# Decode attention backward with one pass over K and V: the query gradient from M = sum of (V row)(p x K row)

## The chip, the cores and the metric

One core of one Trainium2 chip. The time is the device time of that core in microseconds; lower is better. Times of whole kernels are medians of several runs, and each experiment was timed beside runs of the kernel before on the same chip. Views of the profile and landings come from one profiled execution of each kernel. A landing is the moment when one of the 16 DMA engines has finished its share of a transfer; it is read from the semaphore events of the kept trace, which do not name the engine, so landings can only be put in order of time.

## The reference

A transformer layer with one new token per sequence: layer norm, attention over the last 4096 keys of a cache of 32768, output projection, layer norm, gated FFN, and the gradients of all inputs and weights.

```python
# B=2, D=512, Hq=32, Hkv=8, Sk=32768, Dh=128, F=1792; everything bf16
W = min(4096, max(256, Sk // 4)); rep = Hq // Hkv          # 4096 keys, 4 query heads per K/V head
q = (layernorm(x) @ wq).reshape(...)
k = repeat(k_cache[:, :, Sk - W:, :], rep);  v = repeat(v_cache[:, :, Sk - W:, :], rep)
p = softmax(einsum("bhqd,bhkd->bhqk", q, k) * Dh ** -0.5)
h = x + einsum("bhqk,bhkd->bhqd", p, v).reshape(...) @ wo
out = h + (gelu(layernorm(h) @ w_gate) * (layernorm(h) @ w_up)) @ w_down
# results: out, and the gradients of x, k_cache, v_cache, wq, wo, w_gate, w_up, w_down
```

The cache gradients have the cache's full size. Of each, 28672 of 32768 rows are zero, and they must be written: 32 regions of 7.34 MB, 235 MB of zeros.

## The kernel before

Zeros are written by GpSimd's queue from one small tile. Three regions are written by a second routine, which spares one DMA engine in each: 15 rows instead of 16. This is called a sparing below.

```python
SKIP_REGIONS = {6: (0, 1792), 14: (0, 1792), 22: (4, 1792)}     # region: (queue number, rows spared)
def zero_dma(i):                                                # plain: 128 partitions, 16 engines alike
    ...
    nc.gpsimd.dma_start(out=dst, in_=zt[:].unsqueeze(1).to_broadcast([P, nper, ZE]))
def zero_dma_skip(i, q, R=1792):
    ...                                                         # tiny writes that move the engines' order on
    nc.gpsimd.dma_start(out=flat[0:rem0].rearrange("(p k e) -> p k e", p=15, k=kd),
                        in_=zt[0:127:9, :].unsqueeze(1).to_broadcast([15, kd, ZE]))
    ...
```

K is read once for the scores and again for the query gradient:

```python
        def dq_for(bg):                                         # in the dV and dK stage
            Kb = kv_pool.tile([P, NJ, DH], BF16, tag="kv")
            ld_eng().dma_start(out=Kb[:], in_=Kv[:, bg, :, :])  # 1.05 MB, 16 times
            for j in range(NJ):
                c0 = (j // NJH) * NBH + bg * REP
                nc.tensor.matmul(out=dqT_ps[:, bg * REP:(bg + 1) * REP], lhsT=Kb[:, j, :],
                                 rhs=dsT2[:, j % NJH, c0:c0 + REP], start=(j == 0), stop=(j == NJ - 1))
```

V is read once for the output and 10 of its 16 tiles again for dP. All weights are loaded in long runs.

## Time and profile before

| | before |
|---|---|
| time, median (13 runs) | 864.78 us (864.47 to 865.36) |
| profiled span | 863.1 us |
| bytes moved / mean rate | 357.71 MB / 414 GB/s |
| last compute instruction ends / its last store lands | 682 us / 692 us |
| last zero write lands | 861.4 us |
| instructions | 8773 |

The span is a list of bytes at a nearly constant rate, with the compute beside it. The prediction below shows those lines. Two more lines of the page: the queues that fetch instructions (columns: packets, MB, share of 16 engines' time).

```profile
q8 instruction: 29, 0.48, 0.2%
q14 instruction: 12, 0.09, 0.0%
```

### The profile page before, as it was taken

What the parts mean: (1) busy time and instruction counts of PE and PEld (TensorE: products, weight loads), DVE (VectorE), ACT (ScalarE), POOL (GpSimd) and SP (SyncE); (2) the same over time, 40 slices, a digit from 0 to 9 for tenths busy, and PEclk for the clock granted to TensorE, in tenths of its full rate; (3) what the DMA queues carried; (4) which work ended last, traced back from release to release, by engine and by line L of the source; (5) the groups of instructions that cost most, each with busy time, mean ns of one, the idle gap of its engine ahead of it and who ended that gap; (6) DMA issues with size and microseconds to landing.
All of it is one profiled execution on the core that took longest, in us unless ns stands there. A gap on an engine that the chain in (4) does not pass through costs nothing.

```text
span 863.1 us, 8773 instructions
## 1 busy us (share of the span) xinstructions
PE 403.7 (47%) x3691; PEld 227.9 (26%) x3727; DVE 253.6 (29%) x402; ACT 216.3 (25%) x317; POOL 48.2 (6%) x67
## 2 busy tenths in 40 slices
PE   1527863244775949979744555567167200000000
PEld 1415543231543825544312222122032000000000
DVE  2202231000357456423423443567145200000000
ACT  0303441000225415534213333466123100000000
POOL 7000000000110000001010000000000010000000
PEclk9959995556677569976756776798677555555555
DMA  9999999999999999999999999999999999999995
GB/s 362 425 417 420 419 416 416 416 420 423 421 423 424 422 420 420 420 417 422 417 421 419 417 420 424 420 423 422 421 423 425 420 424 425 425 425 425 425 416 218
DMA packets 74809, 357.71 MB, mean 414 GB/s; under 512 B 3977, under 2 KB 3985, under 8 KB 61457
## 3 DMA queue, kind: packets, MB, share of 16 engines
q0 software_dynamic: 58480, 234.89, 72.9%
q1 hardware_dynamic: 13692, 103.38, 30.3%
q10 hardware_dynamic: 2596, 18.88, 5.2%
q8 instruction: 29, 0.48, 0.2%
q14 instruction: 12, 0.09, 0.0%
HBM read 74.72 MB, written 282.33 MB: 414 GB/s over the span
## 4 chain that ended last, share of the span: by engine, by line
another core or an unknown queue 76%; POOL 5%; issue 3%; POOLq 0%
POOL out_dram L107 3%; POOL out_dram L123 0%; POOL out_dram L121 0%; POOL zt L100 0%; POOL out_dram L136 0%; POOL out_dram L132 0%; POOL maskA L152 0%; POOLq L781 0%; POOL maskA L151 0%; POOL pair_f L159 0%; POOL out_dram L126 0%; POOL ident_bf L146 0%; POOL maskC L176 0%; POOL selB L180 0%
## 5 line engine op out<-in xcount | busy, mean ns | idle before, releaser
L70 DVE CAST st<-ps 128x512 bf16<-128x512 f32 (+1 forms) x136 | 92.6, 719 | 90.4 <-ACT st L72 58.5
L72 ACT CAST st<-ps 128x512 bf16<-128x512 f32 (+1 forms) x136 | 80.9, 612 | 105.1 <-PE ps L695 52.9
L301 PE MATMUL KT_ps<-ident_bf,Kb 128*128 128x128 bf16 x832 | 73.1, 234 | 43.8 <-DMA Kb<-in_A_k_cache_dram 42.6
L72 ACT COPY KT_sb<-KT_ps 128x1024 bf16<-128x1024 bf16 x64 | 64.8, 1012 | 104.6 <-PE KT_ps L301 104.6
L301 PEld LDWEIGHTS <-Kb 128*128 128x128 bf16 x832 | 58.4, 105 | 74.5 <-DMA Kb<-in_A_k_cache_dram 45.3
L70 DVE COPY KT_sb<-KT_ps 128x1024 bf16<-128x1024 bf16 x64 | 44.2, 691 | 106.6 <-PE KT_ps L301 89.8
L72 ACT COPY dst<-ps 128x512 bf16<-128x512 bf16 x53 | 31.0, 585 | 125.8 <-PE ps L244 49.7
L695 PE MATMUL ps<-dO_bd,p_bf 128*128 128x512 bf16 x119 | 43.4, 473 | 16.8 <-DVE st L70 15.8
L695 PE MATMUL ps<-Q_bd,ds_bf 128*128 128x512 bf16 x126 | 39.6, 410 | 23.2 <-DVE st L70 22.9
L107 POOL DMA_DIRECT2D out_dram<-zt x29 | 30.8, 1119 | 303.5 <-DMA out_dram<-zt 303.3
L311 PE MATMUL dP_ps<-KT_sb,dOpadX 128*128 128x512 bf16 x116 | 41.2, 430 | 3.8 <-DVE KT_sb L70 2.2
L70 DVE CAST g_st<-ps_gr 128x512 bf16<-128x512 f32 x39 | 26.9, 691 | 44.0 <-PE ps_gr L613 38.6
L311 PE MATMUL S_ps<-KT_sb,QpadX 128*128 128x512 bf16 x115 | 37.3, 397 | 5.0 <-ACT KT_sb L72 4.4
L72 ACT CAST g_st<-ps_gr 128x512 bf16<-128x512 f32 (+1 forms) x39 | 21.2, 544 | 57.4 <-PE ps_gr L613 57.2
L70 DVE COPY dst<-ps 128x512 bf16<-128x512 bf16 x53 | 22.7, 428 | 43.0 <-PE ps L244 31.3
L683 PE MATMUL dqT_ps<-dsT,Kb 128*128 128x4 bf16 x512 | 18.4, 167 | 34.7 <-DMA Kb<-in_A_k_cache_dram 33.7
L683 PEld LDWEIGHTS <-Kb 128*128 128x128 bf16 x512 | 17.4, 102 | 47.1 <-DMA Kb<-in_A_k_cache_dram 38.1
L428 PE MATMUL oT_ps<-pT,Vb 128*128 128x4 bf16 x416 | 13.1, 166 | 33.9 <-DMA Vb<-in_A_v_cache_dram 31.1
L695 PEld LDWEIGHTS <-ds_bf 128*128 128x128 bf16 x128 | 13.1, 102 | 49.7 <-issue 43.2
L244 PE MATMUL ps<-ident_bf,wq_full 128*128 128x128 bf16 x128 | 13.5, 234 | 24.3 <-ACT dst L72 19.8
L695 PEld LDWEIGHTS <-p_bf 128*128 128x128 bf16 x128 | 12.6, 111 | 36.0 <-issue 20.0
L428 PEld LDWEIGHTS <-Vb 128*128 128x128 bf16 x416 | 12.2, 104 | 35.1 <-DMA Vb<-in_A_v_cache_dram 32.1
(201 smaller groups left out, 421.5 us busy)
## 6 DMA issues: line engine op xcount, KB each, us to landing
out_dram<-zt POOLq DMA_DIRECT2D x29, 7168.0 KB, 124.9
Kb<-in_A_k_cache_dram SPq DMA_DIRECT2D x32, 1024.0 KB, 15.8
out_dram<-zt POOLq DMA_DIRECT2D x3, 6720.0 KB, 171.2
out_dram<-st SPq DMA_DIRECT2D x18, 1024.0 KB, 14.8
out_dram<-st ACTq DMA_DIRECT2D x18, 1024.0 KB, 18.1
Vb<-in_A_v_cache_dram SPq DMA_DIRECT2D x13, 1024.0 KB, 11.0
Kb<-in_A_v_cache_dram SPq DMA_DIRECT2D x10, 1024.0 KB, 10.3
out_dram<-g_st SPq DMA_DIRECT2D x5, 1792.0 KB, 15.2
```

The costliest lines, as they stand in the source:

```text
L70: nc.vector.tensor_copy(out=out, in_=in_)
L72: nc.scalar.copy(out=out, in_=in_)
L107: nc.gpsimd.dma_start(out=dst, in_=zt[:].unsqueeze(1).to_broadcast([P, nper, ZE]))
L244: nc.tensor.transpose(out=ps[:, a, :], in_=src_block(a), identity=ident_bf[:])
L301: nc.tensor.transpose(out=KT_ps[:, cc1, jj * P:(jj + 1) * P], in_=Kb[:, j, :], identity=ident_bf[:])
L311: nc.tensor.matmul(out=acc_ps[:, cc, :], lhsT=lhsT, rhs=KT_sb[:, cc1, :], start=(i < 2), stop=(i >= len(units) - 2))
L428: nc.tensor.matmul(out=oT_ps[:, bg * REP:(bg + 1) * REP], lhsT=Vb[:, j, :], rhs=pT2[:, j % NJH, c0:c0 + REP], start=(j == 0), stop=(j == N ...
L683: nc.tensor.matmul(out=dqT_ps[:, bg * REP:(bg + 1) * REP], lhsT=Kb[:, j, :], rhs=dsT2[:, j % NJH, c0:c0 + REP], start=(j == 0), stop=(j == ...
L695: nc.tensor.matmul(out=ps[:, half2, :], lhsT=lhs_bf[:, jp * P:(jp + 1) * P], rhs=rhs_bd[:, half2, bgq * 4:(bgq + 1) * 4, :].rearrange("q g ...
```

## The change

The intent: with delta known only after the output, ds = p(dP - delta), and dq = sum over keys of ds x K. Since dP = V dO, this is M dO - delta x pK, where M = sum over keys of (V row)(p x K row) and pK = sum of p x K. M and pK don't need dO, so they are summed in the same pass as the scores, and K need not come back. The core of the diff (cut; the whole replaces most tile pools by offsets into one tile):

```diff
+        def m_unit(bg, u, M_ps):                               # 4 of the 32 keys of each partition
+            ...
+            for jj in range(4):
+                for i in range(REP):
+                    if jj * REP + i in PK_ON_ACT:              # (2, 5, 8, 11, 14)
+                        nc.scalar.activation(out=pk[:, jj, i, :], in_=Kt[bg][:, j, :], func=ACT.Copy, scale=ef[:, j, i:i + 1])
+                    else:
+                        nc.vector.tensor_scalar(out=pk[:, jj, i, :], in0=Kt[bg][:, j, :], scalar1=ef[:, j, i:i + 1], ...)
+            ...
+                nc.tensor.matmul(out=M_ps[:], lhsT=Vt[bg][:, j, :], rhs=pk[:, jj, :, :]..., ...)
-            Kb = kv_pool.tile([P, NJ, DH], BF16, tag="kv")     # second read of K
-            ld_eng().dma_start(out=Kb[:], in_=Kv[:, bg, :, :])
-        if i in SKIP_REGIONS:
-            zero_dma_skip(i, *SKIP_REGIONS[i])
+        zero_cast(i)                                           # all 32 regions alike
+    wq2 = at(8 * V_SLOT, [P, NDR, HQ * DH], BF16, "wq2")       # wq read a second time
+    nc.sync.dma_start(out=wq2[:], in_=wq_v)
-        3: lambda: nc.sync.dma_start(out=wo_sb[:], in_=A_wo.rearrange("(p r) n -> p r n", r=NOR)),
+    wo_v = A_wo.rearrange("(h d) n -> d h n", h=HQ)            # 1 KB runs; FFN weights and gwd likewise
...
```

V now stays in 12 slots, so 4 tiles are read again in place of 10.

## The prediction

> **What bounds the kernel now.** I read the page first: the rows of slices for the DMA, then the queues and the bytes.
>
> ```profile
> PE   1527863244775949979744555567167200000000
> DVE  2202231000357456423423443567145200000000
> DMA  9999999999999999999999999999999999999995
> ...
> DMA packets 74809, 357.71 MB, mean 414 GB/s; under 512 B 3977, under 2 KB 3985, under 8 KB 61457
> ...
> q0 software_dynamic: 58480, 234.89, 72.9%
> q1 hardware_dynamic: 13692, 103.38, 30.3%
> q10 hardware_dynamic: 2596, 18.88, 5.2%
> ...
> HBM read 74.72 MB, written 282.33 MB: 414 GB/s over the span
> ```
>
> The DMA row is 9 in every slice but the last, while TensorE and VectorE have nothing after slice 33. So the kernel is a list of bytes to be moved: 235 MB of zeros for the untouched part of the two cache gradients (q0, issued by GpSimd) and 122 MB of everything else. The chain of waits says the same in its own way: three quarters of it is "another core or an unknown queue", that is, GpSimd waiting for its zero writes.
>
> Second, the table of stretches (columns: stretch, length, busy time of PE, PEld, DVE, ACT, POOL, granted clock, DMA share, GB/s). I set the borders where the stages change: K scores, V products, FFN, dP with the weight gradients, dV and dK, the last projection, zeros alone, the end.
>
> ```profile
> 0.00:136.00 136.00, 73.00 (x779) 51.32 (x793) 33.52 (x63) 38.73 (x45) 17.10 (x33) 0.87 1.05 410
> 136.00:187.00 51.00, 16.97 (x525) 15.66 (x523) 0.50 (x2) 1.09 (x2) 0.52 (x1) 0.50 1.07 416
> 187.00:300.00 113.00, 73.17 (x730) 50.91 (x731) 43.84 (x81) 33.24 (x45) 10.01 (x11) 0.67 1.15 423
> 300.00:414.00 114.00, 94.14 (x672) 50.52 (x682) 55.61 (x77) 46.00 (x60) 5.83 (x6) 0.82 1.12 421
> 414.00:608.00 194.00, 108.97 (x799) 45.06 (x809) 93.63 (x146) 79.74 (x143) 4.70 (x6) 0.74 1.07 420
> 608.00:690.00 82.00, 37.44 (x193) 14.44 (x192) 26.51 (x37) 17.46 (x24) 4.77 (x5) 0.64 1.11 423
> 690.00:836.00 146.00, 0.00 (x0) 0.00 (x0) 0.00 (x0) 0.00 (x0) 5.30 (x5) 0.50 1.14 425
> 836.00:863.00 27.00, 0.00 (x0) 0.00 (x0) 0.00 (x0) 0.00 (x0) 0.00 (x0) 0.50 0.68 255
> ```
>
> Two things to see. The compute chain ends at 690, so it has some 170 us of slack. And the last 27 us run at 255 instead of 425 GB/s: some DMA engines have finished and others have not, which costs 27 x (1 - 255/425) = 10.8 us.
>
> **What the Trainium skill says.** "DMA: Bandwidth & Descriptors", section "Issuing engines are not separate DMA queues": transfers issued by SP, ACT and GpSimd run on the same 16 engines and interleave. The trace agrees: 410 to 425 GB/s whatever the mix. So a byte not moved anywhere is worth time, as long as the zeros can fill the place. Same page, "Queues, rings and completion order": an engine takes its queues in turn. In the V stage the timeline has one 1 MB tile (1.049 MB) every 3.92 us, 267 of the 416 GB/s, so loads get about two thirds and the zeros still move:
>
> ```profile
> 153.40 1.01 PE L428 MATMUL oT_ps<-pT,Vb 128*128 128x4 bf16 x32 [2.91 <-DMA Vb<-in_A_v_cache_dram]
> 157.35 1.01 PE L428 MATMUL oT_ps<-pT,Vb 128*128 128x4 bf16 x32 [2.94 <-DMA Vb<-in_A_v_cache_dram]
> 161.26 0.93 PEld L428 LDWEIGHTS <-Vb 128*128 128x128 bf16 x32 [2.98 <-DMA Vb<-in_A_v_cache_dram]
> ```
>
> "VectorE: DVE Perf Modes", section "The perf-mode tier table": tensor_scalar on bf16 in SBUF runs at four elements a cycle. The four calls on 128x512 fit:
>
> ```profile
> 134.20 1.14 DVE L410 TENSOR_SCALAR p_bf<-p_bf,rl 128x512 bf16<-128x512 bf16 x4
> ```
>
> Each lasts 350 ns by the groups, so they start (1.14 - 0.35)/3 = 0.263 us apart. "SBUF — State Buffer", section "SBUF: two separate sides", warns that such VectorE modes keep GpSimd from writing descriptors. Before, GpSimd issues a 7 MB zero write in about 1.1 us and has over 100 us of writes queued (the last is issued at 724 and lands at 861), so no run here shows a harm.
>
> **The change part by part.**
>
> *Bytes.* Before, K is read twice (scores, then dq) and V once plus 10 of 16 tiles again for dP. The change computes dq from M = sum over keys of (V row)(p x K row), built in the same pass as the scores, so K is read once; it keeps 12 V tiles and re-reads 4. It gives up keeping wq and reads it again. 357.71 - 16 x 1.049 - 6 x 1.049 + 4.19 = 338.8 MB. At the mean of 414 GB/s that is 818 us, 45 us less than 863.
>
> *Start.* The zero source is set by VectorE as uint32 instead of GpSimd's 1.80 us memset: about -1 us.
>
> *Shorter runs.* wo, the FFN weights and the w_down gradient are now cut into 1 KB runs, 11.5 MB in all. The page's packets are mostly 4 to 8 KB. I choose +5 us, an estimate with no row behind it.
>
> *Balance.* Before, regions 6, 14 and 22 are written so that one engine in each is spared most of its share. One share is 1792 rows x 256 B = 459 KB; at 425/16 = 26.6 GB/s that is 17.3 us, and 16.2 us net, since the spared engine takes a sixteenth of the rest. Engine 0 is spared twice, engine 4 once. The change writes all 32 regions alike. If those engines carry other work (instruction fetches, small transfers), they end later again, up to 32 us; if the sparing overshot, the end becomes more even. Some engines do end early in the 255 GB/s stretch, so it overshot in part. I choose +12 us.
>
> Sum: 818 - 1 + 5 + 12 = 834; the median time stands 1.6 us above the profiled span, so 836 us.
>
> *Does the chain of compute stay inside?* The first pass grows. For each of 16 heads it adds 128 products of a 128x128 tile with a per-row scalar, 88 on VectorE and 40 on ScalarE. From 0.263 us at 512 columns, 384 columns fewer at four per cycle of 0.96 GHz save 0.10 us: 0.16 us each, 88 x 0.16 = 14 us. Two K transposes to copy (0.69 us each in the groups), about ten small softmax operations (2 us) and a copy make 18 us. TensorE: 32 matmuls of 512 columns at 0.22 to 0.43 us, 64 of 128 columns at about 0.08, 32 transposes and 32 score matmuls about 4: 16 to 23 us. So VectorE and TensorE are near each other, 16 x 18 = 290 us at best; with the waits between them I add a quarter, 360, and 25 us of start: it ends near 385, where before scores and V products ended at 187. Then: FFN stage 113, less two round trips of small shuffling DMAs (15.3 us of wait before the attention projection, some 12 us near 300), plus a wait for wo, whose space is free only after the last K tile: 125. dP stage without its V loads: 105 of 114. dV and dK: before, 16.8 MB of K loads and 33.5 MB of stores at two thirds of the rate set the 194 us; stores alone at 280 GB/s take 120. The last projection, without waiting for staging buffers: 60 of 82. Sum 385 + 125 + 105 + 120 + 60 = 795 us, some 40 us inside the 834. So 150 us of slack shrinks, but should not vanish.
>
> **The rivals.**
> (a) *The chain becomes the bound.* For it: the first pass needs some 2,050 small operations where VectorE and ScalarE wait on TensorE and back, and 40 us of margin is 11% of that stage; also the in-order engines have to share them well. Against: the two engines' shares (11 to 5) look tuned. Then the DMA row would have holes at the end and the time would be 845 to 890.
> (b) *One DMA engine ends late* because nothing is spared any more. For it: the deliberate sparing before. Against: no lasting lag is seen before. It would make 840 to 855, with a longer low-rate stretch at the end.
> (c) *The full proportional gain*, small runs free and balance no worse: 817 to 820.
> (d) *Descriptor starvation*: VectorE's fast mode in the first pass slows the zero writes. It would show as a DMA row below 9 there, and cost at most some tens of us; with over 100 us queued I give it little.
>
> **Range and chances.** (c) is the low edge and mild forms of (a) and (b) the high one: 815 to 864. Faster by over 2% means under 847.4. The bytes make that the middle case; (a) or a strong (b) takes a third of the weight away. Slower by over 2%, above 882, needs the first pass at 450 us or more. Chances: 0.67 faster, 0.27 same, 0.06 slower.
>
> **What would show each step.** HBM read near 56 MB and 339 MB in all; the DMA row 9 until the last slice or two; the first pass ending at 360 to 420, VectorE's tensor_scalar groups at about 0.16 us per operation busy; dV and dK in some 120 us; the chain of waits still ending in GpSimd's zero writes. If instead the last instruction group is the wq gradient and the zeros end before it, (a) holds and the number is too low. If the last stretch lies at 200 GB/s or less for over 20 us with compute done, (b). If GpSimd's issues take several us in the first pass and the DMA row dips, (d).

## The result, and the profile after

834.08 us (833.85 to 834.39, 8 runs) against 864.78: the ratio is 0.9645 (0.9636 to 0.9654), so 3.5% faster. A ratio is the mean time of one kernel's fast runs over that of the other's of the same rounds, so it isn't quite the ratio of the medians.

The page after, in the lines that answer to those of before, with the two instruction queues:

```profile
PE   2888988888888897064457688859594657595200
DVE  2799999999999995031145744414694656644200
...
DMA  9999999999999999999999999999999999999994
...
DMA packets 81923, 339.03 MB, mean 407 GB/s; under 512 B 2104, under 2 KB 13888, under 8 KB 72384
...
q8 instruction: 37, 0.61, 0.3%
q14 instruction: 30, 0.25, 0.1%
HBM read 55.84 MB, written 282.33 MB: 406 GB/s over the span
```

The bytes fell by 18.7 MB as worked out. The DMA row is still 9 up to the end, but the mean rate fell from 414 to 407, and VectorE, nearly idle in the first third before, is full there. The table of stretches, cut at the new borders (first pass, FFN, dP with weight gradients, dV and dK, last projection, zeros alone, the end; columns as in the prediction):

```profile
29.00:322.00 293.00, 253.56 (x2606) 119.12 (x2605) 276.48 (x1578) 245.76 (x701) 11.48 (x11) 0.97 1.11 415
322.00:464.00 142.00, 73.13 (x753) 45.21 (x754) 40.44 (x142) 28.70 (x56) 7.30 (x7) 0.65 1.13 408
464.00:602.00 138.00, 104.77 (x751) 57.45 (x765) 63.55 (x93) 56.16 (x75) 6.26 (x6) 0.82 1.12 417
602.00:733.00 131.00, 85.53 (x266) 28.86 (x269) 85.03 (x131) 74.32 (x129) 0.00 (x0) 0.82 1.08 418
733.00:780.00 47.00, 33.42 (x178) 12.53 (x177) 20.16 (x34) 16.87 (x23) 0.00 (x0) 0.72 1.10 421
780.00:814.00 34.00, 0.00 (x0) 0.00 (x0) 0.00 (x0) 0.00 (x0) 0.00 (x0) 0.50 1.13 424
814.00:832.00 18.00, 0.00 (x0) 0.00 (x0) 0.00 (x0) 0.00 (x0) 0.00 (x0) 0.50 0.31 115
```

Compute ends at 778.6, the last store of it lands at 787.2, and the last zero write at 830.5: 43 us of slack where there were some 170. The end stretch has a different form: 18 us at 115 GB/s, where before it was 27 at 255. It loses 18 x (1 - 115/424) = 13.1 us.

The groups of the first pass and the zero writes (busy us, mean ns of one | idle before):

```profile
L340 DVE TENSOR_SCALAR mem<-mem,ef 128x128 bf16<-128x128 bf16 x1408 | 241.3, 254 | 0.0
L338 ACT ACTIVATE mem<-mem,ef 128x128 bf16<-128x128 bf16 x640 | 212.7, 393 | 41.2 <-PE M_ps L351 34.6
L351 PE MATMUL M_ps<-mem 128*128 128x512 bf16 x512 | 184.5, 401 | 28.5 <-DVE mem L340 10.6
...
L112 POOL DMA_DIRECT2D out_dram<-zt x32 | 33.6, 1073 | 562.4 <-DMA out_dram<-zt 562.1
```

241.3/1408 = 0.171 us per scaling: one lasts 254 ns but the next starts before it ends. A zero write is issued in 1.07 us and GpSimd still waits 562 us for its own writes, so the queue never ran dry.

One trap: "the chain that ended last" of this page holds only compute and stores, and no longer GpSimd. That view starts from the last *instruction*, which is now the store of the wq gradient at 779; the last zero write was issued at 598.5 and nothing waits for it. The end of the span is set by landings, and these have to be read from the semaphore events. For the last plain region the sixteen engines land in groups: five at 814.2 to 814.4, nine at 819.2 to 821.0, one at 826.0, one at 830.5.

### The profile page after: what moved, and what is told of

The parts are those of the page before. It is cut to its first block, busy times and chain, and to the rows that moved or that the text cites.

```text
span 832.3 us, 13396 instructions
## 1 busy us (share of the span) xinstructions
PE 562.0 (68%) x4765; PEld 273.5 (33%) x4784; DVE 492.9 (59%) x1996; ACT 427.7 (51%) x991; POOL 36.5 (4%) x52
## 2 busy tenths in 40 slices
DMA packets 81923, 339.03 MB, mean 407 GB/s; under 512 B 2104, under 2 KB 13888, under 8 KB 72384
## 4 chain that ended last, share of the span: by engine, by line
PE 32%; DMA 31%; DVE 22%; ACT 5%; issue 2%; SPq 1%; ACTq 0%; DVEq 0%
DMA out_dram<-mem 19%; DVE mem L340 14%; PE M_ps L351 7%; DMA mem<-in_A_wo_dram 4%; ACT mem L94 4%; DMA mem<-in_B_w_up_dram 3%; PE ps_g L693 3%; DVE mem L92 3%; PE KT_ps L294 3%; DMA mem<-in_A_k_cache_dram 3%; PE ps_tb L220 2%; PE VT_ps L656 2%; PE dP_ps L665 2%; PE ps_gr L602 2%; DMA mem<-in_B_w_gate_dram 2%
## 5 line engine op out<-in xcount | busy, mean ns | idle before, releaser
L340 DVE TENSOR_SCALAR mem<-mem,ef 128x128 bf16<-128x128 bf16 x1408 | 241.3, 254 | 0.0
L338 ACT ACTIVATE mem<-mem,ef 128x128 bf16<-128x128 bf16 x640 | 212.7, 393 | 41.2 <-PE M_ps L351 34.6
L351 PE MATMUL M_ps<-mem 128*128 128x512 bf16 x512 | 184.5, 401 | 28.5 <-DVE mem L340 10.6
L693 PE MATMUL ps_g<-mem 128*128 128x512 bf16 x251 | 84.2, 448 | 50.4 <-ACT mem L94 42.3
L92 DVE CAST mem<-ps_g 128x512 bf16<-128x512 f32 x128 | 83.9, 688 | 44.5 <-PE ps_g L693 38.0
L94 ACT CAST mem<-ps_g 128x512 bf16<-128x512 f32 x128 | 73.7, 586 | 63.3 <-DMA out_dram<-mem 35.1
L351 PEld LDWEIGHTS <-mem 128*128 128x128 bf16 x512 | 48.1, 97 | 114.6 <-DVE mem L340 85.4
L294 PE MATMUL KT_ps<-ident_bf,mem 128*128 128x128 bf16 x512 | 61.3, 229 | 9.1 <-ACT mem L94 8.7
L693 PEld LDWEIGHTS <-mem 128*128 128x128 bf16 x256 | 28.0, 110 | 106.4 <-issue 89.2
L220 PE MATMUL ps_tb<-ident_bf,mem 128*128 128x128 bf16 x424 | 48.2, 253 | 7.3 <-ACT mem L94 5.5
L656 PEld LDWEIGHTS <-mem 128*128 128x128 bf16 x512 | 38.6, 109 | 38.1 <-issue 30.6
L656 PE MATMUL VT_ps<-ident_bf,mem 128*128 128x128 bf16 x512 | 48.4, 241 | 2.2 <-ACT mem L94 1.1
L294 PEld LDWEIGHTS <-mem 128*128 128x128 bf16 x512 | 40.1, 102 | 14.0 <-issue 1.9
L220 PEld LDWEIGHTS <-mem 128*128 128x128 bf16 x424 | 30.7, 109 | 26.6 <-issue 25.7
## 6 DMA issues: line engine op xcount, KB each, us to landing
out_dram<-mem SPq DMA_DIRECT2D x36, 1024.0 KB, 13.1
```

The costliest lines, as they stand in the source:

```text
L92: nc.vector.tensor_copy(out=out, in_=in_)
L94: nc.scalar.copy(out=out, in_=in_)
L220: nc.tensor.transpose(out=ps[:, a, :], in_=src_block(a), identity=ident_bf[:])
L294: nc.tensor.transpose(out=KT_ps[:, jj, :], in_=Kt[bg][:, u * 8 + jj, :], identity=ident_bf[:])
L338: nc.scalar.activation(out=pk[:, jj, i, :], in_=Kt[bg][:, j, :], func=ACT.Copy, scale=ef[:, j, i:i + 1])
L340: nc.vector.tensor_scalar(out=pk[:, jj, i, :], in0=Kt[bg][:, j, :], scalar1=ef[:, j, i:i + 1], scalar2=None, op0=ALU.mult)
```

## The experiments

Code cuts are marked with `...`; the code of the sparing routine, put back where it is used, is left out.

The theory after reading the traces (T): bytes set the time, at some 2.4 us per MB, and the compute has 43 us to spare. Its rivals: the chain of compute sets or nearly sets the end (R1); the lost sparing costs the 12 us that the prediction charged (R2); loads and stores in runs of 1 KB cost nothing (R3). The later runs ask why one engine is late.

### The sparing put back

```diff
+    SKIP_REGIONS = {6: (0, 1792), 14: (0, 1792), 22: (4, 1792)}
-        zero_cast(i)
+        if i in SKIP_REGIONS: zero_dma_skip(i, *SKIP_REGIONS[i])
+        else: zero_cast(i)
```

> The changed kernel with the three skipping regions of the kernel before put back (queue 0 spared in regions 6 and 14, queue 4 in region 22). The prediction charged 12 us for dropping them: by that term alone the time would fall from 834.1 to about 822. The trace after says less: its last 18 us ran at 115 GB/s where 424 was the rate before, which loses about 13.2 us to engines that are done, against about 10.8 us in the kernel before, so putting the sparing back can return about 2.4 us: about 831.5, and the last stretch below 100 GB/s shorter. Rival: the two late engines of the changed kernel are not the two that the old table spares; then 834 to 837 and the same or a longer tail.

Measured: 837.01 us (836.84 to 837.18), 2.9 slower than the change. The landings show why. Three *different* engines came forward, one of the group of five and two of the group of nine, and the late two moved back from 826.0 and 830.5 to 829.0 and 834.1. 3 x 17.3 us spread over the others is 3 to 4 us each. R2 falls, and so does the smaller gain that I expected.

### The kernel before without its sparing

```diff
-SKIP_REGIONS = {6: (0, 1792), 14: (0, 1792), 22: (4, 1792)}
+SKIP_REGIONS = {}
```

> The kernel before with its three sparing regions written plainly. The prediction took it that sparing balances the engines: dropping it would then cost up to 12 us, about 877. In the trace before, three engines end 8 to 17 us ahead of the crowd and one is 3.5 us behind it, so sparing may have moved work onto the crowd, 3 x 17.3 / 13 = 4 us for each of the others: without it about 861 us, with the last landing 3 to 4 us sooner.

Measured: 861.48 us (861.11 to 861.77), 3.2 *faster* than the kernel before, last landing 858.2 in place of 861.4. So the sparing hurt there too: it was aimed at engines that weren't the last. Dropping it is worth 3 us of the change's gain.

### Long runs

```diff
-    wo_v = A_wo.rearrange("(h d) n -> d h n", h=HQ)
+    wo_v = A_wo.rearrange("(p r) n -> p r n", r=HQ)
-        ... B_w_down.rearrange("(r m) n -> m r n", m=P)[:, r0:r0 + nr, :]     # and w_gate, w_up, the gwd store
+        ... B_w_down.rearrange("(m r) n -> m r n", m=P)[:, r0:r0 + nr, :]     # values wrong on purpose
```

> The changed kernel with wo, the three FFN weights and the down-projection gradient moved in long contiguous runs in place of 1 KB runs; bytes are the same, the outputs that depend on these weights are wrong on purpose. If short runs cost what the prediction charged and what the FFN stretch shows (408 GB/s over 142 us against 422 beside it): about 829 us, with packets under 2 KB down from 13888 to below 3000 and slices 13 to 16 of the GB/s row back at 415 to 423. Rival: the fall in that stretch comes from something else (the mix of loads and zero writes, or loads that are waited for) and the time stays at 834.

Measured: 827.86 us (827.66 to 828.01), 6.2 faster; outputs wrong, as intended. Row of GB/s over 40 slices, first the change, then this kernel:

```profile
GB/s 362 414 415 415 414 422 421 421 419 422 422 422 421 398 393 392 393 423 401 402 419 418 422 423 419 416 395 441 406 423 418 415 418 418 416 417 424 420 426 150
```

```profile
GB/s 361 414 416 415 414 421 421 420 423 419 420 422 422 419 419 424 424 415 420 418 423 423 422 419 421 424 420 424 417 415 417 418 415 417 421 424 426 425 418 96
```

```profile
DMA packets 72194, 339.03 MB, mean 410 GB/s; under 512 B 2104, under 2 KB 2112, under 8 KB 62400
```

The dips to 392 and 395 (weights in, gwd, the gradient of w_down, out) are gone. R3 falls. The packets fell from 81923 to 72194.

The landings show more than the time does. The mean of the sixteen last landings came 9.0 us sooner (819.3 to 810.3), but the last engine alone fell further behind the group before it (12.4 us in place of 9.5), so only 6.2 us reached the end.

### The second read of K put back into the change

```diff
+                for _ in range(2):
+                    kx = at((12 + again[0] % 4) * V_SLOT, [P, NJ, DH], BF16, "Kagain")
+                    nc.sync.dma_start(out=kx[:], in_=Kv[:, again[0], :, :])      # nobody reads it
+                    again[0] += 1
```

> The changed kernel with the second read of K put back as sixteen loads of 1.05 MB that nobody uses, into slots of V that are free in the dV and dK stage; results stay correct, no compute is added. If bytes set the time: 16.78 MB more at the 407 to 424 GB/s of that part is 39.6 to 41 us, so 874 to 875 us, with the bytes at 355.8 MB and the zero writes ending later by as much. Rival, the chain of compute sets the end and the reads are hidden: 834 to 845 us. Were the time above 880, the loads would have pushed the stores of that stage past the end of the zero writes.

Measured: 874.00 us (873.86 to 874.12), 39.9 more for 16.78 MB, and results correct. No compute was added.

```profile
DMA packets 84227, 355.81 MB, mean 408 GB/s; under 512 B 2360, under 2 KB 14144, under 8 KB 72640
```

### The second read of K taken from the kernel before

```diff
-            Kb = kv_pool.tile([P, NJ, DH], BF16, tag="kv")
-            ld_eng().dma_start(out=Kb[:], in_=Kv[:, bg, :, :])
-                nc.tensor.matmul(..., lhsT=Kb[:, j, :], ...)
+                nc.tensor.matmul(..., lhsT=dsT2[:, j % NJH, :], ...)             # wrong dq on purpose
```

> The kernel before with only its second read of K taken away (the matmul of dq reads another tile of the same shape; two outputs wrong on purpose), the first pass, the sparing and the long runs as they were. If bytes alone set the time: 340.25 MB at the 414 GB/s of the kernel before is 822 us plus some 2 us of launch, about 824 us, some 10 us better than the whole change, whose rearranged pass then bought nothing but the freedom to drop the reads. Rival, the single pass with its earlier finish matters by itself: 845 to 865 us here.

Measured: 825.68 us (825.66 to 826.06), 39.1 less for 16.8 MB.

```profile
DMA packets 72503, 340.92 MB, mean 414 GB/s; under 512 B 3720, under 2 KB 3728, under 8 KB 61200
```

With the run above: a megabyte is worth 2.33 to 2.38 us, in either structure, and the new pass itself buys nothing but the freedom not to read K again. R1 is hard to hold after these two runs; the next one settles it. Also, this is 8.4 us *better* than the change, which moves 1.9 MB less: by 8.4 + 1.9 x 2.35, the change pays some 13 us for something else.

### VectorE slowed: 3, then 1 of 16 scalings on ScalarE

```diff
-        PK_ON_ACT = (2, 5, 8, 11, 14)
+        PK_ON_ACT = (4, 9, 14)          # first run
+        PK_ON_ACT = (7,)                # second run
```

> The changed kernel with ScalarE doing 3 of the 16 scalings of each group in place of 5, so VectorE does 1664 in place of 1408. At 0.171 us each (241.3 us for 1408 in the trace after) VectorE gets 43.8 us more, all in the first pass, where it is 94% busy. Theory, the transfers set the end and the chain of compute has slack (last store landed at 787, last zero write at 830.5, so 43 us): 834 to 838 us, with the first pass ending near 366 and the last store landing near 830. Rival, the chain of compute sets the end: 834 + 44, about 878 us.

Measured: 834.37 us (834.19 to 834.77), 0.3 more, with the first pass ending at 359 in place of 322. The last store lands at 823.1, 36 us later than in the change, and the time hardly moves: R1 falls.

> The changed kernel with ScalarE doing 1 of the 16 scalings, VectorE 1920: 512 more at 0.171 us are 87.6 us more. Theory (43 us of slack): the last store lands at 787 + 88 = 875, so 875 to 880 us, and the chain is now the bound; first pass ends near 410. Rival, the chain set the end before: 834 + 88, about 922 us. Second rival, a busier VectorE slows the issue of the zero writes: then the GB/s row of the first pass falls below 414 and the issue of a zero write takes more than 1.1 us.

Measured: 853.00 us (851.67 to 857.38), 18.9 more. The first pass ends at 402, 81 later; the last store lands at 849.0, 62 later, and after the last zero write (810.3). Here the chain does set the end, and the time grows by the 62 us less the 43 of slack. So a chain 36 us later is free, and one 62 us later is not: this brackets the slack, whose 43 us are read from the landings. The theory had 875 because it moved every later stage by the same amount. The ends moved by 78 (FFN), 78 (dP), 75 (dV and dK) and 67 us (last projection): 13 us of the difference were won back in the last projection and its stores, probably because the zero writes ran out and the other transfers had the engines to themselves (not tested):

```profile
800.00:850.00 50.00, 36.08 (x208) 14.66 (x207) 26.51 (x44) 23.31 (x34) 0.00 (x0) 0.84 0.45 183
```

The second rival, slower issue: 1.08 us for a zero write, and 416 GB/s in the first pass. Not seen.

### Sixteen sparings in a row

```diff
+    SKIP_REGIONS = {i: (0, 1792) for i in range(6, 22)}
```

> The changed kernel with sixteen regions (6 to 21) written by the sparing code, always with queue number 0. The first experiment showed that two sparings with the same number hit two different transfer engines, and neither of the two late ones. If each sparing moves on by one engine, sixteen of them spare every engine once, 17 us each, and give back nothing: 834 to 837 us, and the landings of each region show at which of the sixteen the latest and the second latest engine jump forward by 17 us. If they hit the same few engines again and again, those end 50 us or more early and the rest carry it: 845 us or more.

Measured: 836.52 us (836.33 to 836.67). Each sparing brought another engine forward, the first of them one of the group of five, the next ones of the group of nine. As I read the landings, the latest came at the twelfth and the second latest at the thirteenth; since landings carry no names, this is a reading and not a measurement. The GB/s row is at 384 to 397 from slice 13 to 21, longer than the dip of the 1 KB runs; probably engines that were ahead ran dry while GpSimd waited for the slowest. So its time pays for more than the sparing.

### Two attempts to spare the late engines

```diff
+    SKIP_REGIONS = {14: (11, 1088), 20: (11, 576)}      # first attempt
+    SKIP_REGIONS = {14: (5, 1792), 20: (5, 576)}        # second attempt
```

> The changed kernel with two sparings aimed at its own two late transfer engines. In the walk over sixteen sparings the latest engine jumped forward at the twelfth and the second latest at the thirteenth, so number 11 in the first sparing and in the second should hit them. The latest lands at 830.5 and the second at 826.0, the other fourteen between 814.2 and 821.0, the mean of all sixteen is 819.4. Sparing 10.5 us of the one (region 14) and 5.6 us of the other (region 20) puts 1 us on the rest: last landing near 822 in place of 830.5, so about 825.5 us. If the numbers hit other engines: 835 to 836 us and a tail as long as before.

Measured: 835.11 us (834.70 to 835.16). Neither late engine was hit. The first sparing brought one of the group of five forward (after it only four land together), the second one of the group of nine. The next expectation has this wrong where it says that both hit the middle group.

> The run before this aimed two sparings at the two late transfer engines and hit two of the middle group: the last landing moved from 830.5 to 831.9. All hits so far (five group with number 0 first, middle group with number 0 second, number 4 third, number 11 first and second) fit a rule in which the engine is the order of the sparing minus the number. By that rule number 5 hits the latest engine as first sparing and the second latest as second. Here: number 5, 17.3 us (region 14), then number 5, 5.6 us (region 20). If the rule holds: the latest goes to 814, the second to 821.5, the other fourteen 1.4 us later, last landing near 822.5, about 826 us. If not: 835 to 837 us, and which engine is late stays unknown.

Measured: 835.53 us (834.89 to 835.73). Again one of the five first and one of the nine second. So both attempts failed, and the rule from queue number to engine is not settled. One pattern stands out: the first sparing of a kernel hit one of the five with the numbers 0, 11 and 5 alike, and the second one of the nine. That fits a rule in which only the order of the sparings counts and the number has no effect; no run tests it.

### More instructions

```diff
         zero_cast(i)
+        for _ in range(80):
+            nc.gpsimd.memset(dummy[:], 0.0)
```

> The changed kernel with 80 one-element memsets on the Pool engine after each issue of a zero write, 2400 in all, where Pool waits 562 us anyway. It asks why one engine is late: the changed kernel has 4600 instructions more than the kernel before (13396 against 8773), and its instruction queues carried 0.86 MB in place of 0.57, 64 bytes an instruction. 2400 more are 0.154 MB. If one transfer engine carries all of them, at the 26.5 GB/s that an engine writes, it ends 5.8 us later: about 840 us, and the last landing 5 to 6 us further behind the crowd. If they are spread over the sixteen: 0.4 us, so 834 to 835 us, and the late engine has another cause. If the memsets hold up the issue of the zero writes, the GB/s row dips between 30 and 600 us and the run says nothing on it.

Measured: 951.03 us (951.02 to 951.14), and as a time this says nothing: nearly all of the memsets ran not between the issues, as I meant, but after about 600, at some seven a microsecond, and the last ended at 949. The landings of the zero writes stay readable. In the last region two landings moved by about 5 us: the latest, from 830.5 to 835.5, and one of the group of five, from 814.4 to 819.1 or a little later. The others are within 0.5 us of the change. Meanwhile the queue of fetches, q14, grew (page of this kernel), with 13 of the new packets before the latest landing:

```profile
q14 instruction: 48, 0.39, 0.1%
```

A packet of 8 KB on q14 takes 0.34 us on average in this trace, so 13 of them are 4.4 us: enough for one of the two shifts, not for both. Which one can be seen. At the end, when only zeros are written, each engine starts a packet every 154 ns, so the engines can be told apart in the packets of the kept trace. Two fetches fall there. The one at 819.9 interrupts none of the seven engines that are still at work, the latest included, so it ran on an engine that was done. The one at 806.3 takes the place of a zero packet in a row that ends at 818.9 and lands at 819.3, not in that of the latest. So the added fetches did not go through the engine that ends last; they fit the one that left the group of five. What moved the latest is open. One hint: from 791 on, 58 of its 283 zero packets took longer than the usual 176 ns, where in the change no packet of that stretch did, so something beside the fetches disturbed it while the memsets ran.

### Fewer instructions

```diff
-            for jj in range(4):
-                for i in range(REP):                              # 16 scalings: 11 tensor_scalar, 5 activation
-                    ...
+            nc.vector.tensor_tensor(out=pk[:, 0:3, :, :],
+                                    in0=Kt[bg][:, j0:j0 + 3, :].unsqueeze(2).to_broadcast([P, 3, REP, DH]),
+                                    in1=ef[:, j0:j0 + 3, :].unsqueeze(3).to_broadcast([P, 3, REP, DH]), op=ALU.mult)
+            for i in range(REP):
+                nc.scalar.activation(out=pk[:, 3, i, :], in_=Kt[bg][:, j0 + 3, :], func=ACT.Copy, scale=ef[:, j0 + 3, i:i + 1])
```

> The changed kernel with the twelve scalings of three of each four keys done by one VectorE multiply of 1536 columns (both inputs spread by broadcast) and the four of the other key on ScalarE: 640 instructions in place of 2048, so 1408 fewer and 90 KB fewer to fetch. By the multiply of 1024 columns in the trace after (1220 ns) one of 1536 takes about 1.83 us, 128 of them 234 us, about the 241 of now, so the chain of compute should stay inside its slack. In the run with 2400 more instructions the latest transfer engine alone came later, by 5.0 us, for 13 more fetches of 8 KB before the zero writes ended; in this kernel 11 fewer should bring it forward by 3.4 to 4 us: last landing near 827, where the second latest engine (826.0) takes over, and the time near 830.5 us. If instruction fetch is not what delays that engine: 834 us. If the large multiplies lengthen the first pass by over 43 us: more than 836 us.

Measured: 830.50 us (830.33 to 830.64), ratio to the kernel before 0.9604 (0.9591 to 0.9617), results correct: the best correct kernel here, 3.6 us under the change. The latest engine lands at 827.1, 3.4 us sooner; five land at 813.9 to 814.3 and ten at 818.1 to 820.9. So the second latest, at 826.0 in the change, has come into the middle group; why, these runs don't say. The run changes two things besides the number of instructions: the bytes fall by 0.09 MB, and the last compute ends 34 us sooner (744.6). Neither explains 3.6 us: 0.09 MB are 0.2 us, and the run with 3 of 16 showed that moving that end by 36 us costs 0.3.

```profile
q14 instruction: 18, 0.15, 0.0%
...
L333 DVE TENSOR_TENSOR mem<-mem,ef 128x1536 bf16<-128x1536 bf16 x128 | 220.1, 1741 | 5.1 <-PE M_ps L347 5.0
```

128 multiplies take 220 us for 1536 scalings, where 1408 took 241 before. Before the last landing there are 11 fetches fewer, and it comes 3.4 us sooner. That fits fetches on the latest engine, which the run above did not bear out; how fewer instructions bring it forward is not shown.

## Why the prediction was right

Right in the mechanism that carries it, and right in the number (836 against 834.1) partly by luck: the sparing was charged 15 us too much, and about 11 us of costs that the prediction did not have made up for it. Term by term:

| term | predicted | shown by runs |
|---|---|---|
| bytes, -18.7 MB | -45 | -44 (2.35 us per MB: both runs with the second read of K) |
| start | -1 | first zero packet at 6.7 in place of 8.0 in the traces; not tested alone |
| 1 KB runs | +5 | +6.2 (long runs) |
| sparing dropped | +12 | -3 (both runs with and without) |
| the latest engine ends further behind | not thought of | about +6 (its lag: 3.4 before without sparing, 9.5 in the change) |
| rest | | about +5, open |

- *Bytes are time.* Right, and it is more than the whole gain. 864.8 - 44 - 3 + 6 + 6 = 830; the change measures 834.1. With 1.3 us for the start the open rest is 5 to 6. The landings give a second account. Against the kernel before without sparing, the mean of the last sixteen landings came 33.2 us sooner (852.5 to 819.3): 45 for the bytes (at the 2.43 us per MB by which both runs with the second read of K moved that mean) less 9.0 for the 1 KB runs leaves about 3 open. The latest engine then stands 11.2 us behind the mean where it stood 5.7. So part of the rest is that the 1 KB runs cost 9 us of engine time and not 6. No run tells the remainder apart.
- *Shorter runs.* Chosen with no row behind it, and near. The run with long runs has 9729 packets fewer; 6.2 us on 16 engines is 10.2 ns of one engine for each, and by the mean of the landings 14.8.
- *Balance.* This step failed. The prediction took a deliberate edit for a working one: "I choose +12 us". The row it showed, engines early by 8 to 17 us in the kernel before, was the sign that the sparing hit the wrong ones, and the prediction did say that it "overshot in part". It overshot altogether. Nor was one engine spared twice, as the prediction read the code: three engines were spared once each. Rival (b), one engine ends late, is half right in its outcome and wrong in its cause: the engine that ends last in the kernel before was not one of the three that come forward.
- *The late engine.* Lag of the latest engine behind the last of the middle group, against the fetches of q14 before the last landing:

| kernel | fetches of 8 KB | lag, us | us per fetch |
|---|---|---|---|
| before | 10 | 3.5 | 0.35 |
| before, no sparing | 10 | 3.4 | 0.34 |
| before, no second read of K | 10 | 5.6 | 0.56 |
| change with one multiply | 18 | 6.2 | 0.34 |
| 3 of 16 on ScalarE | 28 | 12.0 | 0.43 |
| change, K read again | 29 | 8.4 | 0.29 |
| change | 29 | 9.5 | 0.33 |
| long runs | 29 | 12.4 | 0.43 |
| change, 2400 more instructions | 42 | 14.3 | 0.34 |

  The lag grows with the number of fetches, and 1408 instructions fewer took 3.3 us of it away. That is a correlation: with 28 or 29 fetches the lag is anything from 8.4 to 12.4 us, and the two fetches that can be followed did not run on the latest engine. So the missing term of about 6 us is this lag, and its cause stays open, as does what makes the groups of five, nine and one.
- *The chain of compute stays inside.* Right: predicted end about 795 with 40 us to spare, measured 779 (last store 787) with 43, and the slowed kernels agree with it. The stages were further off than the sum. First pass: end 385 predicted, 322 measured. A quarter for waits was added, and VectorE was busy 276 of its 293 us, waiting for almost nothing. FFN 125 against 142, dP 105 against 138, dV and dK 120 against 131: there the new layout waits: the attention projection 27 us for wo, the copies of gradients 44 us in the dP stage and 39 us in the dV and dK stage for staging buffers that were still being stored. Last projection 60 against 47.
- *Scalings* at 0.16 us: 0.171. From 512 to 128 columns the start-to-start time fell by 0.263 - 0.171 = 0.092 us, where the prediction's four elements a cycle gave 0.10.
- *Descriptor starvation* (d), that is, VectorE keeping GpSimd from issuing: not seen, in any run, with up to 1920 scalings on VectorE in the first pass.
- *What would show it.* "The chain of waits still ending in GpSimd's zero writes" was a wrong sign, for the reason given with the profile after. A reader going by it would have found rival (a) confirmed, which the slowed kernels refute.

## What to carry to other kernels

Where the transfer engines are full from end to end, price a change by its bytes first (here 2.35 us per MB), then by its packets (here 10 to 15 ns of one engine each), and try it with fewer instructions (here 1408 fewer gave 3.6 us, by a way not shown). Look at the landings of each engine and not only at the rate: the last one sets the time. A hand-tuned balance in the old kernel is a claim to be tested by removing it, not a cost of losing it. Many small operations in a fast mode can be worse than one large one in a slow mode: a scaling starts every 171 ns for 128 columns, which is 2.05 us for twelve, against 1.74 for one multiply of 1536, with a twelfth of the instructions.

## What the Trainium skill lacked or had wrong

- "Runtime: NRT & Kernel Launch", section "Instruction fetch mechanics", has the blocks at 16 KiB and the cost of a block as one tail-bump, mostly hidden. The traces show two kinds: q8 in packets of 16 KB (37 x 16 KB is, by arithmetic, TensorE's instructions at 64 bytes), q14 in packets of 8 KB (by the same arithmetic those of the other engines), which take 0.33 us each in the change. Whether their cost is hidden in a kernel bound by transfers is not settled: 1408 instructions fewer went with 3.6 us, but the fetches that can be followed did not delay the engine that ends last.
- "DMA: Bandwidth & Descriptors", section "Specifications", lists some 358 GB/s as the limit of HBM for a core. This core alone held 414 GB/s of HBM traffic in the kernel before and 406 in the change, by the page's HBM line. The skill is not wrong here, for a note under its bandwidth table says that the 358 are for two cores streaming together; the row in "Specifications" doesn't say so.
- "VectorE: DVE Perf Modes", section "The perf-mode tier table", is for 2048 columns. At 128 columns tensor_scalar starts every 171 ns, of which four elements a cycle at the page's 0.96 GHz would be 33 (an estimate from the page); the fixed part decides. The page does warn elsewhere that each instruction pays a fixed cost; the table alone does not show it. The multiply of bf16 by float32 took 1741 ns for 1536 columns, which agrees with the table's float32 row (2293 ns for 2048, so 1720 by proportion, an estimate from the page).
- No page was found that says which DMA engine carries an instruction fetch. On the engines of a transfer with 15 rows, "DMA: Bandwidth & Descriptors" has a rule, consecutive engines from a cursor that goes round; the first sparing hit one of the five early engines whatever its number was, and four sparings aimed at the two late engines hit neither. No run here tests the page's rule.
